# Transposing q of five attention units with VectorE instead of TensorE, from loads by 32x32 blocks

## The chip, the cores and the metric

The kernel runs on one core of one Trainium2 chip. The metric is the device time of that core in microseconds (us), lower is better. A profile shows one execution; its span is some 2 us shorter than the time.

## The reference

Retention attention, then a feed-forward block with a product of two projections, all in float32.

```python
# q, k, v: (8, 8, 576, 64)
scores = q @ k.transpose(0, 1, 3, 2) / sqrt(64)
ret = scores * Dmat                  # Dmat[h, i, j] = gamma[h] ** (i - j) for i >= j, else 0
attn = ret @ v                       # then (B, H, S, D) -> x of (B*S, H*D) = (4608, 512)
out = ((x @ w1) * (x @ w2)) @ w3 @ w_out
```

## The kernel before

The batch is worked on in four pairs. A pair has five units of tokens: a short one of 64 and four of 128. Units are numbered 0 to 19; units 5 to 9 are the second pair and unit 10 is the short one of the third. For each unit TensorE (PE) makes scores from q and k with the head dimension on the partitions, so both must be transposed. The decay is put on q and v by a multiplication on GpSimd.

Before the change, units 0 to 10 took this path: one load per tensor, transposes on PE into PSUM (tp), copies by ScalarE. In all code below, "..." marks what is left out.

```python
def front(g, names="kq"):
    for nm in names:
        src = live[nm, g]
        dst = pools["fr"].tile([P, 2, NP, P], F32, tag=nm + "T", ...)
        for b in range(2):
            tp = acc.tile([P, NP, P], F32, tag="acc", name="tp")
            for p in range(NP):                       # NP = 4: 8 transposes in all
                ...
                nc.tensor.transpose(tp[:, p, :sz], src[:sz, h:h + 2, :]..., ident[:sz, :sz])   # L228
            nc.scalar.copy(dst[:, b, :, :sz], tp[:, :, :sz])                                   # L231
        live[nm + "T", g] = dst
```

Units 11 to 19 took another one, for q and k alike. The loads put every 32x32 block where it has to end up, and VectorE transposes inside the blocks, from SBUF to SBUF.

```python
def load_blocks(g, nm):            # 16 DMAs of 32 KB for a full unit, 8 for the short one
    ...
    t = pools["ld"].tile([P, 2 * NP, P // BL, BL], F32, tag="ld_q", name="bl_" + nm)   # shares two buffers with ld_q
    ...
    for a in range(2):
        for f in range(D // BL):                      # BL = 32
            ...
            for m in range(n):
                ...
                nc.sync.dma_start(t[part:part + BL, :, m, :], src[a, :, s0:s0 + BL, ...])      # L181
def scale_blocks(g): ...           # two GpSimd multiplications by the decay                   # L191
def front_blocks(g):
    ...
    for nm in "kq":
        ...
        nc.vector.transpose(dst..., live["bl_" + nm, g][:, :, :n, :])                          # L200
```

Between the parts of a unit the kernel puts pieces of the feed-forward work: "up" (products up, additions c on VectorE) and "down" (products po, additions ot on VectorE, then a store of the result).

Of the kernel before, what the change touches and what calls it, by code (L numbers as in the profile page):

```python
# [40 lines left out]
def kernel(  # L41
# [27 lines left out]
    NC = (S + P - 1) // P  # L69
# [24 lines left out]
    def open_attention(part):  # L94
        for nm in ("ld", "fr"):
            pools[nm] = part.enter_context(
                tc.tile_pool(name=nm, bufs=2, side="right", reuse_waits="tile"))
# [9 lines left out]
    def load(g, names, engine=nc.sync):  # L107
        i, c = divmod(g, NC)
        sz = sizes[c]
        src = {"k": k, "q": q, "v": v}  # L110
        for nm in names:
            t = pools["ld"].tile([P, 2 * H, D], F32, tag="ld_" + nm, name="ld_" + nm)
            engine.dma_start(
                t[:sz], src[nm][2 * i:2 * i + 2, :, starts[c]:starts[c] + sz, :].rearrange("b h p d -> p (b h) d"))
            live[nm, g] = t
# [54 lines left out]
    def load_blocks(g, nm):  # L170

        i, c = divmod(g, NC)
        n = sizes[c] // BL
        t = pools["ld"].tile([P, 2 * NP, P // BL, BL], F32, tag="ld_q", name="bl_" + nm)
        src = {"k": k, "q": q}[nm][2 * i:2 * i + 2].rearrange("b (p a) s d -> a (b p) s d", a=2)
        for a in range(2):
            for f in range(D // BL):
                part = (a * (D // BL) + f) * BL
                for m in range(n):
                    s0 = starts[c] + m * BL  # L180
                    nc.sync.dma_start(t[part:part + BL, :, m, :],  # L181
                                      src[a, :, s0:s0 + BL, f * BL:(f + 1) * BL].rearrange("m r x -> r m x"))
        live["bl_" + nm, g] = t

    def scale_blocks(g):
        c = g % NC
        n, n0 = sizes[c] // BL, starts[c] // BL
        t = live["bl_q", g]
        for b in range(2):
            part = t[:, b * NP:(b + 1) * NP, :n, :]  # L190
            nc.gpsimd.tensor_tensor(  # L191
                out=part, in0=part, in1=gqs[:, :, n0:n0 + n].unsqueeze(3).to_broadcast([P, NP, n, BL]),
                op=ALU.mult)

    def front_blocks(g):
        c = g % NC
        n = sizes[c] // BL
        for nm in "kq":
            dst = pools["fr"].tile([P, 2, NP, P], F32, tag=nm + "T", name=nm + "T", bufs=1 if nm == "k" else 2)
            nc.vector.transpose(  # L200
                dst[:, :, :, :sizes[c]].rearrange("p b m (n x) -> p (b m) n x", x=BL),
                live["bl_" + nm, g][:, :, :n, :])
            live[nm + "T", g] = dst

    def scale(g, nm, scalar=False):
        c = g % NC
        sz = sizes[c]
        t, gam = live[nm, g], {"q": gq, "v": gk}[nm]
        t = t[:sz].rearrange("p (b h) d -> p b h d", b=2)
        if scalar:  # L210
            for h in range(H):
                nc.scalar.mul(t[:, :, h, :], t[:, :, h, :], gam[:sz, c, h:h + 1])
            return
        nc.gpsimd.tensor_tensor(  # L214
            out=t, in0=t, in1=gam[:sz, c].unsqueeze(1).unsqueeze(3).to_broadcast([sz, 2, H, D]), op=ALU.mult)

    def front(g, names="kq"):
        c = g % NC
        sz = sizes[c]
        for nm in names:  # L220
            src = live[nm, g]
            dst = pools["fr"].tile([P, 2, NP, P], F32, tag=nm + "T", name=nm + "T",
                                   bufs=1 if nm == "k" and g >= NC else 2)
            for b in range(2):
                tp = acc.tile([P, NP, P], F32, tag="acc", name="tp")
                for p in range(NP):
                    h = b * H + 2 * p
                    nc.tensor.transpose(tp[:, p, :sz],  # L228
                                        src[:sz, h:h + 2, :].rearrange("p a d -> p (a d)"),
                                        ident[:sz, :sz])  # L230
                nc.scalar.copy(dst[:, b, :, :sz], tp[:, :, :sz])  # L231
            live[nm + "T", g] = dst

    def score(g):
        c = g % NC
        sz = sizes[c]
        kT, qT = live["kT", g], live["qT", g]
        pm = pools["fr"].tile([P, 2, 2, NP, P], F32, tag="pm", name="pm", bufs=1)
        for b in range(2):
            sc = [acc.tile([P, NP, P], F32, tag="acc", name="sc") for j in range(2)]  # L240
            for p in range(NP):
                for j, hs in enumerate(heads):
                    nc.tensor.matmul(sc[j][:sz, p, :sz], kT[hs, b, p, :sz], qT[hs, b, p, :sz],  # L243
                                     start=True, stop=True)
            for j in range(2):
                nc.vector.tensor_mul(pm[:sz, b, j, :, :sz], sc[j][:sz, :, :sz],  # L246
                                     mask[:sz, :sz].unsqueeze(1).to_broadcast([sz, NP, sz]))
        live["pm", g] = pm

    def state(g):  # L250
        c = g % NC
        sz = sizes[c]
        if c == NC - 1:
            return
        vs = live["v", g]
        kn = live["k", g]
        if c == 0:
            live["st"] = st_ps.tile([P, 2, NP, D], F32, tag="st", name="st")
        st = live["st"]

        for b in range(2):
            for p in range(NP):
                for j, hs in enumerate(heads):
                    h = b * H + 2 * p + j
                    nc.tensor.matmul(st[hs, b, p, :], kn[:sz, h, :], vs[:sz, h, :],  # L265
                                     start=(c == 0 and b == 0 and p == 0), stop=(c == NC - 2),
                                     skip_group_check=True)
        sb = pools["fr"].tile([P, 2, NP, D], F32, tag="sb", name="sb")
        nc.scalar.copy(sb, st)
        live["sb", g + 1] = sb  # L270
# [486 lines left out]
    carry(2, 2)  # L757
    weights_part.close()
    open_attention(ctx)
    for g in (NC, NC + 1):  # L760
        load(g, "kqv")
    keep_stores.clear()
    store()
    todo = [(down, (0, 0), (0, 1)), (down, (1, 0), (1, 1)), (down, (0, 2), (1, 2))]
# [18 lines left out]
    def work(n):  # L783
        for _ in range(min(n, len(todo))):
            fn, *args = todo.pop(0)

            nxt = next((x for x in todo if x[0] is not carry), None)
            if nxt and nxt[0] is down and fn is not carry:
                if fn is down:
                    args.append(nxt[1:])  # L790
                else:
                    last = args == [*every[max(nxt[1][0], nxt[2][0])], NQ - 1]
                    ahead(*nxt[1:], 1 if last else 3)
            fn(*args)
# [3 lines left out]
    front(NC)  # L798
    state(NC)
    score(NC)  # L800
    scale(NC + 1, "q")
    in_blocks = [u > 2 * NC for u in range(G)] + [False] * 2
    for g in range(NC, G):
        c = g % NC
        n = -(-len(todo) // (NC - c))
        if g + 2 < G and not in_blocks[g + 2]:
            load(g + 2, "kq")
        if g + 1 < G:
            scale(g + 1, "v")
            if not in_blocks[g + 1]:  # L810
                front(g + 1)
        half = (n + 1) // 2
        if in_blocks[g + 1]:
            scale_blocks(g + 1)
            work(1)
            front_blocks(g + 1)
            half = max(half - 1, 0)
        if in_blocks[g + 2]:
            load_blocks(g + 2, "q")
            load_blocks(g + 2, "k")  # L820
        work(half)
        pv(g)

        if g + 2 < G:
            queue = nc.scalar if in_blocks[g + 2] else nc.sync
            load(g + 2, "v", queue)
            if in_blocks[g + 2] and (g + 2) % NC != NC - 1:
                load(g + 2, "k", queue)
        if g + 1 < G:
            state(g + 1)  # L830
            score(g + 1)
        if g + 2 < G and not in_blocks[g + 2]:
            scale(g + 2, "q")
        if g == NC + 1:
            strassen_tokens(1, 0)
            todo.extend((up, 1, 0, fp) for fp in range(2))
        work(n // 2)
        if c == NC - 1:
            add_pair(g // NC)
# [44 lines left out]
```

## Time and profile before

| | before |
|---|---|
| time, median of 6 runs | 869.64 us (868.48 to 870.07) |
| span of the profile | 867.5 us |
| PE busy | 845.7 us |
| VectorE busy | 468.0 us |
| ScalarE busy | 185.9 us |
| GpSimd busy | 115.3 us |

How to read it: PE is busy 97% of the span, so the other engines' sums matter only where PE waits for them.

### The profile page before, as it was taken

The numbers are of one execution on the slowest core, as the hardware profiler recorded it, in microseconds if no ns is written. First come the engines' busy times: TensorE is split into PE (matmuls) and PEld (weight loads), VectorE is DVE, ScalarE is ACT, GpSimd is POOL, SyncE is SP. The second block draws the span as 40 slices with busy tenths as digits, with TensorE's granted clock in tenths as the row PEclk, the third lists the DMA queues.
The fourth block names the chain that finished last, engine by engine and source line by source line (L and its number), as shares of the span: only waits on it lengthen the run. The fifth ranks groups of instructions, "written<-read, shape, count | busy, mean of one in ns | idle before, by whom it ended". The sixth has DMA issues, their size and how long they took to land.

```text
span 867.5 us, 15264 instructions
## 1 busy us (share of the span) xinstructions
PE 845.7 (97%) x6309; PEld 771.2 (89%) x6309; DVE 468.0 (54%) x789; ACT 185.9 (21%) x374; POOL 115.3 (13%) x91
## 2 busy tenths in 40 slices
PE   5899999999999999999999999999999999999998
PEld 5889999544888999999999999999999999999996
DVE  4799998986643334543544443534553435334343
ACT  3666333343122221101011101111101100011000
POOL 3010020001202223202023030230400101000000
PEclk9999999999999999999999999999999999999999
DMA  9993453444235534516142335061300000000001
GB/s 192 227 212 115 99 98 98 122 139 74 43 91 125 113 47 81 96 27 110 32 88 39 64 59 95 28 114 24 58 25 26 1 25 1 25 25 1 25 1 48
DMA packets 194628, 63.19 MB, mean 73 GB/s; under 512 B 176632, under 2 KB 184824, under 8 KB 194560
## 3 DMA queue, kind: packets, MB, share of 16 engines
q1 hardware_dynamic: 161920, 54.07, 29.9%
q10 hardware_dynamic: 32640, 8.16, 5.0%
q8 instruction: 49, 0.80, 0.4%
q14 instruction: 19, 0.16, 0.1%
HBM read 52.76 MB, written 9.44 MB: 72 GB/s over the span
## 4 chain that ended last, share of the span: by engine, by line
PE 86%; DVE 7%; DMA 3%; issue 2%; ACT 1%; SPq 1%; POOL 0%; DVEq 0%; ACTq 0%; POOLq 0%
PE up L497 46%; PE po L603 24%; PE ps L452 4%; PE sc L243 4%; PE xps L300 3%; PE xps L293 2%; PE tp L228 2%; PE st L265 1%; DVE c L502 1%; DMA ld_q<-in_q_dram 1%; DVE e L391 1%; DMA ld_k<-in_k_dram 1%; DVE w L402 1%; DVE pm L246 1%; DVE m L377 1%
## 5 line engine op out<-in xcount | busy, mean ns | idle before, releaser
L502 DVE TENSOR_TENSOR c<-up,c 128x384 f32<-128x384 f32 x240 | 133.3, 555 | 187.5 <-PE up L497 182.3
L497 PE MATMUL up<-xT,wA 128*128 128x192 f32 x1152 | 213.0, 328 | 1.1 <-ACT xT L305 1.1
L497 PEld LDWEIGHTS up<-xT,wA 128*128 128x128 f32 x1152 | 191.8, 191 | 3.6 <-ACT xT L305 1.4
L497 PE MATMUL up<-T,wS 128*128 128x192 f32 x768 | 141.4, 327 | 3.3 <-DVE T L471 2.1
L497 PEld LDWEIGHTS up<-T,wS 128*128 128x128 f32 x768 | 127.8, 191 | 3.8 <-issue 2.4
L603 PE MATMUL po<-w3o,ab 128*128 128x256 f32 x456 | 104.4, 381 | 0.8 <-DVE ab L569 0.5
L603 PEld LDWEIGHTS po<-w3o,ab 128*128 128x128 f32 x456 | 85.8, 190 | 13.1 <-DVE ab L569 0.9
L607 DVE TENSOR_TENSOR ot<-po,ot 128x256 f32<-128x256 f32 x90 | 38.2, 424 | 74.6 <-PE po L603 71.8
L517 ACT COPY c<-up 128x384 f32<-128x384 f32 x48 | 22.9, 477 | 225.9 <-PE up L497 221.7
L497 PE MATMUL up<-xT,wS 128*128 128x192 f32 x384 | 70.7, 327 | 0.6 <-DVE c L502 0.5
L246 DVE TENSOR_TENSOR pm<-sc,mask 128x512 f32<-128x512 f32 (+1 forms) x80 | 45.4, 628 | 46.6 <-PE sc L243 46.6
L497 PE MATMUL up<-T,wA 128*128 128x192 f32 x384 | 70.3, 326 | 0.0
L603 PE MATMUL po<-wB,forms 128*128 128x256 f32 x288 | 65.1, 379 | 0.0
L497 PEld LDWEIGHTS up<-xT,wS 128*128 128x128 f32 x384 | 63.5, 190 | 1.7 <-DVE c L502 1.7
L497 PEld LDWEIGHTS up<-T,wA 128*128 128x128 f32 x384 | 63.7, 190 | 0.0
L214 POOL TENSOR_TENSOR ld_v<-ld_v,gk 128x1024 f32<-128x1024 f32 (+1 forms) x17 | 33.1, 1949 | 213.0 <-DMA ld_v<-in_v_dram 187.9
L603 PEld LDWEIGHTS po<-wB,forms 128*128 128x128 f32 x288 | 54.7, 190 | 7.4
L452 PE MATMUL ps<-wo,w3T 128*128 128x512 f32 x128 | 56.1, 596 | 2.9 <-DVE w3T L406 2.9
L452 PEld LDWEIGHTS ps<-wo,w3T 128*128 128x128 f32 x128 | 23.8, 190 | 34.4 <-issue 30.6
L471 POOL TENSOR_TENSOR T<-xT,T 128x384 f32<-128x384 f32 x20 | 20.9, 1043 | 214.3 <-PE up L497 212.5
L523 DVE TENSOR_TENSOR ab<-c 128x768 f32<-128x768 f32 x48 | 46.5, 968 | 3.8
L510 ACT COPY c<-up 128x384 f32<-128x384 f32 x48 | 22.8, 476 | 117.3 <-PE up L497 68.4
(73 smaller groups left out, 805.8 us busy)
## 6 DMA issues: line engine op xcount, KB each, us to landing
raw<-in_moe_w_dram SPq DMA_DIRECT2D x64, 128.0 KB, 3.0
out_dram<-ot SPq DMA_DIRECT2D x24, 256.0 KB, 2.1
bl_q<-in_q_dram SPq DMA_DIRECT2D x136, 32.0 KB, 2.1
bl_k<-in_k_dram SPq DMA_DIRECT2D x136, 32.0 KB, 2.2
raw<-in_moe_w_dram SPq DMA_DIRECT2D x8, 512.0 KB, 7.3
raw<-in_moe_w_dram SPq DMA_DIRECT2D x16, 256.0 KB, 5.7
ld_k<-in_k_dram SPq DMA_DIRECT2D x8, 512.0 KB, 6.9
ld_q<-in_q_dram SPq DMA_DIRECT2D x8, 512.0 KB, 8.5
```

What stands on the lines that cost most here:

```text
L214: nc.gpsimd.tensor_tensor(out=t, in0=t, in1=gam[:sz, c].unsqueeze(1).unsqueeze(3).to_broadcast([sz, 2, H, D]), op=ALU.mult)
L243: nc.tensor.matmul(sc[j][:sz, p, :sz], kT[hs, b, p, :sz], qT[hs, b, p, :sz], start=True, stop=True)
L246: nc.vector.tensor_mul(pm[:sz, b, j, :, :sz], sc[j][:sz, :, :sz], mask[:sz, :sz].unsqueeze(1).to_broadcast([sz, NP, sz]))
L300: nc.tensor.matmul(banks[r][heads[half], b, n, :sz], vs[:sz, b * H + 2 * p + j, :], pm[:sz, b, j, p, :sz], start=(c == 0 and m == 0), stop ...
L452: nc.tensor.matmul(ps, live["w3T", ft][:, g, :], live["wo"][:, g, :], start=(g == 0), stop=(g == KF - 1))
L497: nc.tensor.matmul(ps[:, w, :], a[:, w, r, :], b[:, r, :], start=(new and w == r == 0), stop=(w == r == 1), skip_group_check=True)
L502: nc.vector.tensor_add(c[:, to], ps, c[:, sb])
L510: nc.scalar.copy(c[:, 0], p1)
L517: nc.scalar.copy(c[:, 0], p1)
L523: nc.vector.tensor_mul(ab[:, 4 * fp:4 * fp + 4, :], c[:, :, 0, :], c[:, :, 1, :])
L603: nc.tensor.matmul(ps[nm], a[A][:, f, :], live["W"][B][:, f, :], start=(f == 0 and not on), stop=(f == NP - 1), skip_group_check=True)
L607: nc.vector.tensor_add(ot[:, to[0], to[1]], ps[nm], ot[:, sb[0], sb[1]])
```

## The change

The intent: q of units 6 to 10 takes the block path, so that PE, which has no idle time there, is rid of half of the transposes. k stays with PE.

```diff
-    def front_blocks(g):
+    def front_blocks(g, names="kq"):
...
-        for nm in "kq":
+        for nm in names:
...
-    for g in (NC, NC + 1):
-        load(g, "kqv")
+    load(NC, "kqv")
+    load(NC + 1, "kv")
+    load_blocks(NC + 1, "q")
...
-    scale(NC + 1, "q")
+    scale_blocks(NC + 1)
...
-            load(g + 2, "kq")
+            load(g + 2, "k")
+            load_blocks(g + 2, "q")
...
-                front(g + 1)
+                front(g + 1, "k")
+                front_blocks(g + 1, "q")
...
-            scale(g + 2, "q")
+            scale_blocks(g + 2)
```

NC is 5, so NC + 1 is unit 6; the lines with g + 1 and g + 2 stand in the loop over units and cover the rest.

## The prediction

> **What bounds the kernel now.** I read the page's busy shares first, then the chain of waits cut to 240 to 320 us, where the five changed units lie, then the busy time of each engine in stretches, and last the timeline of single instructions, for the slack of the other engines.
>
> The page says that TensorE (PE) is busy nearly throughout:
>
> ```profile
> span 867.5 us, 15264 instructions
> PE 845.7 (97%) x6309; PEld 771.2 (89%) x6309; DVE 468.0 (54%) x789; ACT 185.9 (21%) x374; POOL 115.3 (13%) x91
> ```
>
> The stretches (busy us and count of each engine, clock, DMA share, GB/s) say where it is not: 17.5 us are lost before 230 us and 4 us after 850 us. Between, and wherever this change touches, PE has next to no idle time, so each microsecond of PE work taken out should come off the end.
>
> ```profile
> 0.00:230.00 230.00, 212.48 (x1469) 174.02 (x1469) 190.57 (x334) 100.84 (x190) 25.51 (x20) 0.99 0.63 134
> 230.00:320.00 90.00, 89.88 (x889) 81.45 (x890) 35.82 (x63) 21.55 (x49) 17.56 (x12) 1.00 0.42 88
> 320.00:560.00 240.00, 240.00 (x1965) 228.57 (x1964) 112.13 (x182) 29.98 (x65) 46.54 (x38) 1.00 0.36 66
> ```
>
> The chain of waits in the changed part (start, length, what) is PE alone, piece against piece:
>
> ```profile
> 260.03 1.99 PE sc L243 x32
> 262.02 1.90 PE tp L228 x16
> 263.91 12.09 PE po L603 x56
> ...
> 317.60 0.98 PE tp L228 x16
> 318.58 1.50 PE up L497 x8
> ```
>
> The 16 tp are the 8 transposes of k and the 8 of q of the next unit. A full unit's 16 hold PE for 1.90 us, the short unit's 16 (64 rows) for 0.98 us. Two more pairs of 1.90 us stand at 281.85 and 301.68 us, and the first at 243.89 us.
>
> **What the Trainium skill says.** "VectorE: DVE Perf Modes", section "The three transpose paths", says that VectorE transposes within 32x32 blocks only and writes to SBUF, where TensorE does a full 128x128 into PSUM. The trace agrees with both halves: PE's transposes are followed by ScalarE copies (L231), VectorE's are not, and the loads that feed VectorE (L181) place each 32x32 block where it will be wanted. "TensorE: Matmul & The Clock Gate", section "Part 4: PE-mode transpose", gives some 275 ns for one transpose inside a kernel. The mean record here is 295 ns, but they overlap: 16 take 1.90 us, 119 ns each. The cost on the path is 119 ns. "DMA: Bandwidth & Descriptors", section "Bandwidth", warns that transfers under 64 KB are dominated by descriptors. The block loads are 32 KB and sixteen of them took 9.29 us to issue, so this case agrees; it is the main danger to look at.
>
> **The change part by part.** Units 6 to 9 are full (128 tokens), unit 10 is the short one that begins the third pair. For each, q takes the path that units 11 to 19 take now; k and v stay.
>
> Removed from PE: 8 transposes of q in each of 5 units. By the chain, half of 1.90 us four times and half of 0.98 us once: 3.80 + 0.49 = 4.29 us. By start times, from the first q transpose to the next product (262.88 to 263.75 us, and so on: 0.87, 0.87, 0.87, 0.88 and 0.59 us), 4.08 us. I take the middle, **4.2 us**, all of it on the path.
>
> Removed from ScalarE: 10 copies (603 ns, or 382 ns for the short unit), 5.6 us. ScalarE is 24% busy here and not on the chain: worth nothing.
>
> Added to VectorE: 5 transposes. Four by 1202 ns and one by 671 ns are 5.5 us:
>
> ```profile
> L200 DVE STREAM_TRANSPOSE qT<-bl_q 128x1024 f32<-128x1024 f32 x8 | 9.6, 1202 | 0.0
> ```
>
> VectorE is 40% busy between 230 and 320 us. The order of its instructions puts each transpose just behind the four masked products (L246) of the unit before it. In the three units where a "down" block follows, the next VectorE instruction then has been waiting for PE:
>
> ```profile
> 269.13 0.69 DVE L628 TENSOR_TENSOR ab<-ab,forms 128x512 f32<-128x512 f32 x1 [5.50 <-PE po L603]
> ```
>
> 5.50 us of idle time take 1.2 us. Where an "up" block follows (units 9 and 10) the idle time before the first addition is 2.98 and 2.27 us; with PE coming some 0.9 or 0.5 us earlier there remain about 0.9 us (2.98 - 0.9 - 1.2) and 1.1 us (2.27 - 0.5 - 0.7). PE itself still has spare accumulators there. Hidden.
>
> Added to the queue on SyncE: sixteen issues of 32 KB (eight for the short unit) in place of one of 512 KB. GpSimd scales q in two halves of 1226 ns in place of one of 2092 ns. When is q ready, and when does VectorE come for it? I use these lines of the timeline, of unit 8's load today and of the block load of unit 11:
>
> ```profile
> 262.93 2.23 SPq L113 DMA_DIRECT2D ld_q<-in_q_dram  x1
> 270.13 1.90 POOL L214 TENSOR_TENSOR ld_q<-ld_q,gq 128x1024 f32<-128x1024 f32 x1 [2.51 <-DMA ld_q<-in_q_dram]
> 316.39 9.29 SPq L181 DMA_DIRECT2D bl_q<-in_q_dram  x16
> ```
>
> Estimate: issue start + 9.3 us + 2.1 us landing (the page) + 2.5 us of scaling, 13.9 us in all. Unit 7: 243.5 + 13.9 = 257.4, wanted when the masked products end at 263.6. Unit 8: 262.9 + 13.9 = 276.8, wanted at 283.5. Unit 9: 280.9 + 13.9 = 294.8, wanted at 303.3. Unit 10, half as long: 300.8 + 4.7 + 2.1 + 1.2 = 308.8, wanted at 319.2. Unit 6 is loaded from about 215 and wanted at 245. The wanted times come up to 4 us earlier as PE gains, but the load starts (set by PE freeing k's buffer) come with them, so at most about 1 us of these 6 to 14 us is lost. The same queue sends results at 256.6, 274.8 and 294.6 us, and would be through with q at 252.8, 272.2 and 290.2. Nothing is displaced.
>
> Sum: 4.2 us gained on PE, nothing added on the path. 869.5 - 4.2 = **865.3 us**, 0.5% faster.
>
> **The rivals.**
>
> First, q comes late: the 32 KB loads meet k and v on the same queue and DMA engines. For: sixteen bl_k at 325.8 us took 14.01 us, of which 6.4 us was a wait for another load's completion, because completions are counted on eight semaphores in turn. Against: 14 us instead of 9.3 us would leave unit 7, the tightest, with about 0.5 us; and then VectorE, not PE, would stand, with 5 us more before PE needs it. To cost time the load has to be later than the worst one of this trace by several microseconds. I put 1 in 10 on it; it would eat 1 to 5 us, ending at 866 to 870 us.
>
> Second, VectorE becomes the bound for a moment where a transpose stands ahead of the additions that free accumulators. For: the remaining idle time before the "up" additions is only about 1 us. Against: the lag of one 1.2 us transpose is made up within three products (1.30 us of PE against 0.56 us of VectorE each). It would cost under 1 us in total.
>
> Third, the gain is given back later: PE arrives 4 us earlier at the block-loaded units, where at 562 us VectorE's transposes are on the chain and PE waits 0.2 us. For: 72 DMAs in place of 5 shift which of the eight semaphores each later transfer takes, so unit 11's k may wait for one more neighbour. Against: these loads are started by PE's own progress and move with it, and from 320 to 560 us PE shows no idle time at all. I allow 0 to 1 us.
>
> A gain above 4.3 us would need something other than the transposes: PE has no idle time there to win.
>
> **Range and chances.** The three runs before span 1.2 us, so the two medians alone make about 0.6 us of doubt; the size of the PE term makes 0.2; the rivals lean to the slow side. The range is 864.2 to 867.0 us. A change of 2% is 17 us: four times all that the removed work is worth, and a loss of that size would need a stall at every unit. Chances: faster 0.01, same 0.98, slower 0.01.
>
> **What would show it right or wrong.** In the chain after the change, tp pieces at these five places should read x8 and about 0.95 us (0.5 us for the short unit), and "po" or "up" should follow at once. PE's busy sum should fall by 4 to 5 us, VectorE's rise by 5.5 us, ScalarE's fall by 5.6 us. The first block products after unit 10 (L243, today at 353.3 us) should start about 4.2 us earlier. Wrong would be: PE idle time released by the L200 transpose or L246 between 240 and 320 us (rival one); a longer wait of PE on the additions L502 there (rival two); the 4.2 us present at 350 us and gone by 570 us (rival three); or single transposes that cost PE more or less than 119 ns when only k's eight remain.

## More of the kernel before

The output tile ot has one buffer, and stores go through SyncE's queue, as the loads do.

The prediction shows the chain of waits in the part concerned. Two more of its lines serve as marks in what follows: the start of the last three products of the weights w3 and w_out (ps), just ahead of the changed part, and the last block of products. Columns are start, length and what ran. Chain of the kernel before:

```profile
197.58 20.97 PE ps L452 x48
854.95 8.91 PE po L603 x40
```

From the one to the other are 657.37 us. All that the change touches lies between these marks, and what varies from run to run ahead of 197 us does not.

## The result, and the profile after

The changed kernel took 865.12 us (median of 6, 864.07 to 865.51) against 869.64 us (6 runs, 868.48 to 870.07). The ratio is 0.995, interval 0.9937 to 0.9962. By the 2% verdict that is the same time; the difference itself is clear of the noise. The output is correct.

From the page of the changed kernel:

```profile
span 862.4 us, 15290 instructions
PE 840.2 (97%) x6269; PEld 764.8 (89%) x6269; DVE 473.8 (55%) x794; ACT 181.6 (21%) x364; POOL 115.3 (13%) x96
```

PE lost 40 instructions and 5.5 us of busy time, VectorE gained five instructions and 5.8 us, ScalarE lost ten and 4.3 us. The chain of the changed kernel shows where:

```profile
196.90 20.98 PE ps L452 x48
...
258.27 1.99 PE sc L243 x32
260.26 1.02 PE tp L228 x8
261.28 12.09 PE po L603 x56
...
313.22 0.48 PE tp L228 x8
...
850.05 8.91 PE po L603 x40
```

The tp pieces are x8 instead of x16, and the next products follow with no gap. Between the marks are now 850.05 - 196.90 = 653.15 us, **4.22 us less**. The span differs by 5.1 us, but 0.68 us of that was there at the first mark, where both programs have done the same instructions, and 0.2 us lie behind the last one; these parts are taken as chance.

Comparing chain against chain, the lead of the changed kernel over the one before is 0.89 us when the short unit 5 is scored, and then grows by 0.87, 0.87, 0.88, 0.87 and 0.50 us at the five places, to 4.88 us. It is still 4.88 us at the products at 560 us, where the prediction feared for it, and 4.90 us at the last block.

The timeline of the changed kernel shows the added work beside PE. Columns are start, length, engine, line and operation, tiles with their sizes, count, and in brackets the idle time ahead with what ended it:

```profile
242.60 9.88 SPq L181 DMA_DIRECT2D bl_q<-in_q_dram  x16
254.44 2.51 POOL L191 TENSOR_TENSOR bl_q<-bl_q,gqs 128x512 f32<-128x512 f32 x2 [22.42 <-PE po L603]
261.80 1.23 DVE L200 STREAM_TRANSPOSE qT<-bl_q 128x1024 f32<-128x1024 f32 x1
266.50 0.69 DVE L628 TENSOR_TENSOR ab<-ab,forms 128x512 f32<-128x512 f32 x1 [3.47 <-PE po L603]
301.91 0.56 DVE L502 TENSOR_TENSOR c<-up,c 128x384 f32<-128x384 f32 x1 [0.96 <-PE up L497]
```

Unit 7's q is issued in 9.88 us and scaled at 256.95 us, 4.9 us before VectorE comes to it at 261.80. After the transpose VectorE still waits 3.47 us for PE. The smallest remainder is the 0.96 us ahead of an "up" block.

One thing in the trace was not looked for. GpSimd scales q and v of unit 6 just when VectorE makes the sums for the first down block, and VectorE's operations become long:

```profile
229.41 2.61 POOL L214 TENSOR_TENSOR ld_v<-ld_v,gk 128x1024 f32<-128x1024 f32 x1
230.30 2.27 DVE L573 TENSOR_TENSOR forms<-ab 128x512 f32<-128x512 f32 x1
```

This sum takes 0.69 us elsewhere. It starts 0.9 us into GpSimd's multiplication and ends 0.55 us after it. The kernel before has the same meeting some microseconds earlier, with another operation of VectorE, one that takes 1.22 us elsewhere:

```profile
221.97 2.74 POOL L214 TENSOR_TENSOR ld_v<-ld_v,gk 128x1024 f32<-128x1024 f32 x1 [0.23 <-DMA ld_v<-in_v_dram]
...
223.34 2.46 DVE L540 TENSOR_TENSOR wB<-w3o 128x1024 f32<-128x1024 f32 x1
```

The Trainium skill, "SBUF — State Buffer", section "Who interferes with whom", has the rule: a VectorE instruction with two SBUF inputs contends with a GpSimd instruction that reads SBUF, for ports that only one of them can hold at a time. Both pairs of lines agree with it: VectorE came second and ended 0.55 and 1.09 us after GpSimd, not much less than the 0.69 and 1.22 us that its operations take elsewhere. From the first mark to the transposes of unit 5 this stretch takes 43.16 us before and 42.96 us after. So 0.2 us of the 4.22 us gained come from this stretch, where the meeting is the difference that the trace shows, and 4.0 us from the transposes.

### The profile page after: what moved, and what is told of

Same layout as the page of the kernel before. It is cut to its first block, busy times and chain, and to the rows that moved or that the text cites. A ratio compares the mean times of both kernels' runs of the same rounds, so it can differ in the third digit from the quotient of the medians.

```text
span 862.4 us, 15290 instructions
## 1 busy us (share of the span) xinstructions
PE 840.2 (97%) x6269; PEld 764.8 (89%) x6269; DVE 473.8 (55%) x794; ACT 181.6 (21%) x364; POOL 115.3 (13%) x96
## 4 chain that ended last, share of the span: by engine, by line
PE 85%; DVE 7%; DMA 4%; issue 2%; ACT 1%; SPq 1%; POOL 0%; DVEq 0%; ACTq 0%; POOLq 0%
PE up L497 46%; PE po L603 24%; PE ps L452 4%; PE sc L243 4%; PE xps L300 3%; PE xps L293 2%; PE st L265 1%; DVE c L502 1%; DMA ld_q<-in_q_dram 1%; PE tp L228 1%; DMA raw<-in_moe_w_dram 1%; DVE e L391 1%; DMA ld_k<-in_k_dram 1%; DVE w L402 1%; SPq L725 0%
```

## The experiments

Theory: PE's time on q's transposes is the whole gain, and loads, scaling and VectorE's transposes are hidden. Rivals: part of the gain is eaten by loads, GpSimd or VectorE; or part of it comes from ScalarE's relief. The kernel before ran beside every kernel on the same chip. "Mark to mark" is the time from the first ps mark to the last block in the run's trace (657.37 us before, 653.15 us after); "to unit 5" is the time from that ps mark to unit 5's transposes.

| run | median us | ratio to before (interval) | mark to mark us | to unit 5, us |
|---|---|---|---|---|
| e1_bound | 864.36 | 0.9946 (0.9934 to 0.9959) | 652.34 | 42.16 |
| e4_keep_pe | 869.22 | 0.9999 (0.9986 to 1.0012) | 657.12 | 42.95 |
| e2_twice_dve | 863.78 | 0.9945 (0.9932 to 0.9957) | 653.14 | 42.94 |
| e3_split | 870.35 | 1.0014 (1.0001 to 1.0028) | 659.63 | 42.15 |
| e5_split6 | 863.09 | 0.9935 (0.9922 to 0.9948) | 652.34 | 42.16 |
| e6_k_blocks | 877.76 | 1.0098 (1.0078 to 1.0118) | 664.42 | 42.96 |
| e7_k_first | 877.54 | 1.0101 (1.0085 to 1.0117) | 663.64 | 42.16 |
| e8_split_act | 868.11 | 0.9983 (0.9965 to 1.0000) | 656.83 | 42.15 |
| after_again | 864.09 | 0.9945 (0.9931 to 0.9959) | 653.13 | 42.95 |
| e5_again | 863.91 | 0.9941 (0.9927 to 0.9955) | 652.32 | 42.15 |
| e9_k7to10 | 864.94 | 0.9962 (0.9942 to 0.9981) | 656.33 | 42.16 |
| e10_k10 | 863.74 | 0.9939 (0.9927 to 0.9951) | 651.83 | 42.14 |

The changed kernel run again gives 653.13 us mark to mark, against 653.15; the run with only unit 6's loads split, repeated, 652.32 against 652.34. This measure repeats to a few hundredths in these two pairs, while the first mark itself stood anywhere from 195.53 to 199.04 us.

**q's transposes gone, with nothing in their place** (wrong result):

```diff
# kernel before
-                front(g + 1)
+                front(g + 1, "k", twice=True)   # ScalarE copies k's transpose to kT and to qT
# and no load and no scaling of q for units 6 to 10
```

> q's transposes of units 6 to 10 are dropped and nothing is put in their place: no load of q, no scaling, no VectorE transpose; ScalarE copies k's transpose a second time as q's (the output is wrong on purpose). This bounds what the change can win. Theory (PE's transposes are the whole gain, everything added is hidden): the same as the changed kernel within 1 us, some 0.9950 to 0.9955 of before, and in the chain each tp piece x8 with 1.02 us. Rival (part of the gain is eaten by the loads by blocks, GpSimd or VectorE): this run is faster than the changed kernel by over 1 us, 0.9935 or less of before.

Measured: 0.9946, a little under the expected 0.9950 to 0.9955 and well above the rival's 0.9935; 652.34 us mark to mark, 0.81 us less than the changed kernel, within the expected 1 us. Of that, 0.80 us lie in the stretch to unit 5, where GpSimd has no q to scale and does not meet VectorE. From unit 5 to the end it takes 652.34 - 42.16 = 610.18 us, the changed kernel 653.15 - 42.96 = 610.19 us. So at the five places the additions cost nothing, and the one price of the change that is seen is the meeting at unit 6.

**The PE work put back:**

```diff
# changed kernel
                 front(g + 1, "k")
+                # 8 transposes of k again, into accumulators that nobody reads
                 front_blocks(g + 1, "q")
```

> The changed kernel with 8 more transposes of k on PE at each of the five places, into accumulators that nobody reads: all that the change adds, without what it removes from PE. Theory: the time of the kernel before comes back, 4.0 us over the changed kernel, ratio to before 0.999 to 1.001, tp pieces x16 with 1.90 us. Rival (a part of the gain came from ScalarE's ten copies fewer, or from other loads): the ratio stays at 0.998 or less.

Measured: 0.9999, as expected. Mark to mark it is 3.97 us above the changed kernel. That settles the size, and that ScalarE's ten copies fewer are worth nothing. Chain of this run (L819 are the added transposes):

```profile
262.61 1.02 PE tp L228 x8
263.63 0.87 PE tp L819 x8
```

The first eight in a row cost 1.02 us and the second eight 0.87 us. Halving the pair of 1.90 us, as one of the two estimates of the prediction did, takes too much for what the second eight are worth.

**VectorE's transposes done twice:**

```diff
# changed kernel, front_blocks, for q of units 6 to 10
                 nc.vector.transpose(dst..., live["bl_" + nm, g]...)
+                nc.vector.transpose(dst..., live["bl_" + nm, g]...)
```

> The changed kernel with each of VectorE's five transposes of q done twice, 5.8 us more of VectorE work at the same places. Theory (they fall into time in which VectorE waits for PE): within 0.7 us of the changed kernel, ratio to before 0.995; the idle time ahead of the next VectorE instruction falls from 3.5 to 2.2 us. Rival (VectorE is at its limit there): 1 to 5 us slower than the changed kernel, PE idle time released by L502 or L628.

Measured: 653.14 us mark to mark, 0.01 us from the changed kernel. In the timeline the additions of the "down" block still wait for PE:

```profile
267.22 0.69 DVE L632 TENSOR_TENSOR ab<-ab,forms 128x512 f32<-128x512 f32 x1 [2.19 <-PE po L607]
```

VectorE is not at its limit there, even where only 0.96 us were left ahead of an "up" block.

**Each load of q as two of half the size:**

```diff
# changed kernel, load_blocks, for q of units 6 to 10
-                    nc.sync.dma_start(t[part:part + BL, :, m, :], ...)          # 32 KB
+                    for h in range(2):                                          # 16 KB each
+                        nc.sync.dma_start(t[part:part + BL, hp, m, :], ...)
```

> The changed kernel with each 32 KB load of q for units 6 to 10 issued as two of 16 KB: the same bytes, twice the issues. Theory (slack of 4 to 5 us at the tightest unit, and 3.5 us more before PE needs VectorE): a unit's issues take 15 to 19 us, unit 7 is scaled at 262 to 266 us instead of 257, VectorE waits up to 4 us at 261.8, PE little: the changed kernel's time plus 0 to 1.5 us. Rival (lateness of the load goes straight to the end): 3 to 8 us slower, PE idle time at units 7, 8 and 9.

Measured: 1.0014; mark to mark 6.48 us above the changed kernel, though it gains the 0.8 us at unit 6. The theory's expectation (0 to 1.5 us) was wrong here, and the rival's size was right. The timeline of this run shows a way to PE that was not thought of:

```profile
241.46 18.57 SPq L183 DMA_DIRECT2D bl_q<-in_q_dram  x32
260.12 1.74 SPq L651 DMA_DIRECT2D out_dram<-ot  x3
264.27 0.37 ACT L628 COPY ot<-po 128x256 f32<-128x256 f32 x1 [3.45 <-DMA out_dram<-ot]
264.69 1.99 PE L606 MATMUL po<-w3o,ab 128*128 128x256 f32 x8 [1.09 <-ACT ot L628]
```

SyncE issues for 18.57 us. The results of the down block, which were ready at about 256 us, go out at 260.12. ScalarE may not write the one output tile before they have left, and PE may not add to the accumulator that ScalarE has to copy. So PE waits at a place that has nothing to do with q. This happens twice, for 1.09 and 2.71 us; a third wait, 0.99 us at unit 9, is for VectorE's additions behind a late q. After the longest wait the granted clock of PE is 0.50 for 3.4 us, and the first eight products take 3.32 us instead of 1.89 us.

**The same with the result stores on ScalarE's queue:**

```diff
# the run before this one
-            nc.sync.dma_start(*stores.pop(0))
+            (nc.scalar if act_stores else nc.sync).dma_start(*stores.pop(0))   # true in the iterations of units 5 to 8
```

> The run with every q load split in two, with the result stores of these iterations issued by ScalarE's queue instead of SyncE's. Theory (what that run lost came of the stores queued behind q's loads, with one output buffer that ScalarE could not refill, and not of q itself being late): no wait of L628 on the store, the time returns to the changed kernel's plus 0 to 2 us, ratio to before 0.994 to 0.998. Rival (q's lateness is what costs, VectorE's wait for it reaching PE): the loss stays, ratio 1.000 or more.

Measured: 0.9983, 656.83 us mark to mark. That is 2.80 us better than with the stores behind q, and still 4.5 us over the run that splits unit 6's loads alone (652.34). So the stores account for a part of the loss. The rest begins with q itself: in this run SyncE's queue issues q for 17.4 to 19.1 us of every full unit, and a unit of the changed kernel takes 277.23 - 258.27 = 18.96 us. The lateness adds up from unit to unit, until VectorE waits too long, and PE for VectorE:

```profile
283.53 19.13 SPq L183 DMA_DIRECT2D bl_q<-in_q_dram  x32
...
306.17 1.25 DVE L203 STREAM_TRANSPOSE qT<-bl_q 128x1024 f32<-128x1024 f32 x1 [6.75 <-POOL bl_q L194]
309.23 2.52 PE L500 MATMUL up<-xT,wS 128*128 128x192 f32 x8 [2.61 <-DVE c L505]
```

A wait of PE costs more than its length here. The stretch just behind this one, in the view by windows (the third figure from the end is the granted clock):

```profile
309.70:313.10 3.40, 3.40 (x35) 2.96 (x37) 1.35 (x3) 0.00 (x0) 0.15 (x1) 0.50 0.20 30
```

At a clock of 0.50 these 3.4 us do the work of 1.7 us (an estimate). With the wait of 2.61 us that makes 4.3 of the 4.5 us. All five runs in which PE stood still for 2.5 us or more between the marks (e3, e6, e7, e8, e9) have such a stretch, 3.4 to 10.2 us long, and the other traces have none there; so part of what these five lost is clock and not waiting.

Both the theory's and the rival's account hold in part. The expected range (0 to 2 us over the changed kernel) was missed: mark to mark it is 3.68 us over it.

**Only unit 6's loads split**, so that they land later:

```diff
# changed kernel
-    load_blocks(NC + 1, "q")
+    load_blocks(NC + 1, "q", split=2)
```

> The changed kernel with only unit 6's loads of q split in two, so that they land some 8 us later and GpSimd scales q and v at 234 to 238 us instead of 226 to 232. Theory (GpSimd's scaling beside VectorE's sums for the down block stretches these from 0.69 and 0.95 us to 2.3 and 1.8 us, on the chain): the stretch from PE's last w3 product (ps) to its first transpose of unit 5 shortens by 0.8 us, as in the two runs before where GpSimd was idle there (42.15 us against 42.96), the forms sum is back at 0.69 us, and the ratio to before is about 0.994. Rival (those VectorE durations are not GpSimd's doing, or the later load delays unit 6): no change or a loss.

> Unit 6's loads split, again. Theory (GpSimd's scaling out of VectorE's way is worth 0.8 us): 0.8 us, 0.1%, under the changed kernel of the same rounds, which the interval may not tell; in the trace 42.15 us from the last w3 products to unit 5's transposes.

> The changed kernel again, unaltered, on the chip and in the rounds of the next three: 0.995 of before.

Measured: 42.16 and 42.15 us to unit 5, against 42.96 and 42.95 us for the changed kernel in its two traces. VectorE's sum is back at its length, and GpSimd comes after it:

```profile
227.70 0.69 DVE L576 TENSOR_TENSOR forms<-ab 128x512 f32<-128x512 f32 x1
...
232.87 2.06 POOL L194 TENSOR_TENSOR bl_q<-bl_q,gqs 128x512 f32<-128x512 f32 x2 [17.61 <-DMA bl_q<-in_q_dram]
```

GpSimd's scaling, 3.35 us in the changed kernel, takes 2.06 us at this later time. The 0.8 us are shown in the traces. It is not the loads that slow VectorE: in the run with k first (e7, below) SyncE issues sixteen loads from 214.12 us on, as in the changed kernel, GpSimd scales later, and the stretch takes 42.16 us. The medians of the same rounds (863.91 against 864.09 us) cannot tell them: the intervals overlap almost wholly.

**k by blocks as well**, to see whether the other half of the transposes can go the same way:

```diff
# changed kernel
+    load_blocks(NC + 1, "k")                                # unit 6, SyncE's queue, behind q
...
-            load_blocks(g + 2, "q")
...
-                front(g + 1, "k")
-                front_blocks(g + 1, "q")
+                front_blocks(g + 1)
+        if g + 2 < G and not in_blocks[g + 2]:
+            load_blocks(g + 2, "q")                         # now behind the transposes of unit g + 1
...
         work(half)
+        if g + 2 < G and not in_blocks[g + 2]:
+            load_blocks(g + 2, "k", nc.scalar)              # units 7 to 10, ScalarE's queue
         pv(g)
```

> The changed kernel with k of units 6 to 10 by blocks too (units 7 to 10 issued by ScalarE's queue after its copies of the down block): the other half of the transposes. Theory (each eight transposes are worth what PE spends on them, as long as loads and VectorE keep their slack): no tp pieces after unit 5, 4.0 to 4.6 us less than the changed kernel, ratio to before 0.990. Rival (VectorE, with two transposes in a row, or k's late landing puts PE to waiting): less than 2 us gained, PE idle time released by L200, L246 or L502 between 240 and 320 us.

> The same with unit 6's k loaded ahead of its q, which moves GpSimd's scaling from 226 to about 234 us. Theory of the collision: 0.8 us less than the run with q first, ratio to before 0.989; rival: the same time.

Measured: 1.0098, and 1.0101 with k first. Both are misses. The block tiles share two buffers with q of unit 5, which PE transposes at 238.5 us; unit 6's second block load had to wait for that. The timeline of the run with q first:

```profile
239.74 8.85 SPq L181 DMA_DIRECT2D bl_k<-in_k_dram  x16
...
250.56 1.25 DVE L200 STREAM_TRANSPOSE kT<-bl_k 128x1024 f32<-128x1024 f32 x1 [7.85 <-DMA bl_k<-in_k_dram]
```

VectorE waits 7.85 us for k, and PE stands 8.1 us at one place, 7.5 us with k first. What holds PE there is, as in the run with twice the issues, the results: their stores stood in SyncE's queue behind the sixteen loads. The timeline with k first names them:

```profile
253.13 0.37 ACT L625 COPY ot<-po 128x256 f32<-128x256 f32 x1 [11.01 <-DMA out_dram<-ot]
253.55 3.78 PE L603 MATMUL po<-w3o,ab 128*128 128x256 f32 x8 [7.49 <-ACT ot L625]
```

With q first the view puts ScalarE's wait down to VectorE's transpose, which ended within 0.2 us of the last store's landing; there the two are not told apart. Of the worth of k's transposes the two runs say nothing. With k loaded first the stretch to unit 5 again took 42.16 us, as expected for GpSimd's scaling at a later time, and mark to mark this run is 0.78 us shorter than the one with q first, against 0.8 us expected; the two medians cannot tell that.

**k of units 7 to 10 by blocks, unit 6's k left on PE** (and unit 6's q split):

> The same with k of units 7 to 10 by blocks as well, units 7 to 9 on ScalarE's queue, unit 6's k left on PE (in the two runs before, its load had to wait for a buffer until 238 us). Theory (each further eight transposes are worth 1.0 us while loads keep pace): up to 3.5 us under the run with unit 6's loads split, ratio 0.990. Rival (a second set of 16 loads per unit does not fit into the 18 us of a unit, whichever queue issues it): slower than that run, PE idle time behind VectorE's transposes or ScalarE's copies.

The edit is that of the k runs above, without the load of unit 6's k by blocks and with unit 10's k on SyncE's queue. Measured: 0.9962, 656.33 us mark to mark, 4.0 us over the run without k. The loads on ScalarE's queue take 10.4 to 10.9 us to issue and can begin only after ScalarE's copies of the down block; VectorE waits about 5 us for k at each full unit:

```profile
252.06 10.70 ACTq L183 DMA_DIRECT2D bl_k<-in_k_dram  x16
...
286.24 1.25 DVE L203 STREAM_TRANSPOSE kT<-bl_k 128x1024 f32<-128x1024 f32 x1 [4.74 <-DMA bl_k<-in_k_dram]
```

The transposes that PE no longer makes are gone, and PE waits instead, 3.0 us at the longest (for VectorE's additions at unit 9), with 3.4 us at a clock of 0.50 behind it. The rival's account holds for this arrangement. Whether another one, with more buffers and an earlier start, could hide k's loads stays open.

**k of unit 10 alone**, on SyncE's queue (and unit 6's q split):

```diff
# run with unit 6's loads split
+        if g + 2 == 2 * NC:
+            load_blocks(g + 2, "k")             # 8 DMAs; front_blocks(10) then takes both
```

> The same with k of unit 10 alone by blocks, on SyncE's queue, where the short unit leaves eight free places. Theory: the tp piece at 313 us goes, 0.5 us more gained, ratio 0.993, no new idle time of PE. Rival: VectorE's two transposes ahead of the up block's additions cost as much as PE gains.

Measured: 651.83 us mark to mark, 0.50 us under the mean of the two runs with unit 6's loads split (652.33), as expected. The chain goes from the scores straight to the products:

```profile
311.49 1.99 PE sc L246 x32
313.48 9.30 PE up L500 x56
```

Of all the versions this one is the shortest mark to mark: 1.31 us under the changed kernel and 5.54 us under the one before. Its median of 863.74 us against 864.09 us in the same rounds lies within the noise, so only the trace calls it better than the changed kernel.

## Why the prediction was right

- **The PE term.** Predicted 4.2 us, between 4.08 and 4.29 us. The five places gave 3.99 us, and putting the transposes back cost 3.97 us. The way by start times was the better one; the halves of the chain's pieces overrate the second eight. Together with 0.2 us from the meeting of GpSimd and VectorE, which the prediction did not see, the trace gives 4.22 us. That the total agrees so closely is partly luck. Two of the signs that the prediction named did not come out as written: k's eight transposes cost 1.02 us, 127 ns each, where 119 ns stood, and PE's busy sum fell by 5.5 us instead of 4 to 5 us. Of these, 1.4 us lie ahead of the first mark; between the marks it fell by 4.1 us.
- **ScalarE.** Predicted 5.6 us less, worth nothing. The copies of q by themselves fell from 10.9 to 5.8 us, 5.1 us, and the engine's busy time by 4.3 us; the rest is not accounted for. That it is worth nothing was shown by the run with the PE work put back.
- **VectorE.** Predicted 5.5 us more, hidden; 5.8 us were measured, and twice as much was hidden too. The remainders worked out for the "up" blocks, 0.9 and 1.1 us, came out as 0.96 and 1.15 us.
- **The loads.** From the first issue to the end of the scaling the prediction had 13.9 us for units 7, 8 and 9 and 8.0 us for unit 10; the trace has 14.35, 14.19, 15.00 and 7.35 us (unit 7: 256.95 - 242.60). From there to VectorE's coming were 4.9, 5.0, 6.6 and 8.4 us, and 14.5 us for unit 6. (The prediction's own sums give 6.2 to 10.4 us for units 7 to 10 and some 16 us for unit 6, so its "6 to 14" is a slip.) "Nothing is displaced" holds as well: the stores after unit 7's loads began at 254.88 us, and the last load was issued at 252.48. But between q and the stores the queue had only 2.4, 0.9 and 2.0 us left at units 7, 8 and 9, where the prediction had 3.8, 2.6 and 4.4.
- **The step that was off.** The first rival said that a late load would meet VectorE first, with 5 us more before PE needs it. The run with twice the issues shows that SyncE's stores reach PE sooner, through the single output tile, and that lateness adds up over the units. The chance given to it did not matter, since the loads were not late; the margin was smaller than the prediction made it: it allowed for 14 us of issuing and 5 us on top, and with 18.57 us of issuing at unit 7 PE already waited 1.09 us.
- **The step that was missing.** The prediction looked at what GpSimd's scaling costs GpSimd, not at what it does to VectorE beside it. At unit 6 that costs 0.8 us of what the change could have won.
- **Given back later?** No. The lead is 4.88 us at 350 us, 4.88 us at 560 us and 4.90 us at the end.

## What to carry to other kernels

Where one engine is gap-free, the worth of work taken off it is read from the distance of starts on that engine, not from instruction records: here 109 ns for a transpose whose record says about 293 ns. Then ask of everything added not only whether it lands in time, but which queue it stands in and what else stands behind it there: q had at least 4.9 us to spare, and the results behind it in the same queue as little as 0.9 us. And when runs differ by more than the effect, take the time between two marks in the trace that enclose the change.

## What the Trainium skill lacked or had wrong

- "TensorE: Matmul & The Clock Gate", Part 4, gives one transpose as some 390 ns alone and 275 ns in a kernel. It lacks the cost in a row: eight float32 transposes of 128x128 hold PE for 1.02 us, a second eight behind them for 0.87 us, which is 109 ns each.
- "VectorE: DVE Perf Modes", "The three transpose paths", gives VectorE's transpose for one 128x128 bf16 tile (311 ns). It has no float32 figure: 128x1024 float32 took 1.21 us here, 151 ns for each 128 columns.
- "SBUF — State Buffer", "Who interferes with whom", has the rule for VectorE and GpSimd, and it held. It lacks a float32 example of the price to both: a sum of 0.69 us took 2.27 us, GpSimd's two multiplications 3.35 us instead of 2.06 us, and PE lost 0.8 us.
- "DMA: Bandwidth & Descriptors" calls transfers under 64 KB descriptor-dominated. It has no figure for what the issuing queue pays for such loads: in the traces here sixteen of 32 KB for q took 7.7 to 11.8 us of SyncE, thirty-two of 16 KB 17.4 to 20.5 us; so about 0.5 to 0.7 us each, whichever of the two sizes.
